# Side work admitted by an estimated clock of three engines instead of fixed allowances, in an attention and GLU block

## The chip, the cores and the metric

The kernel runs on 1 core of one Trainium2 chip. The metric is the device time of one execution in microseconds (us). A core has five engines that run side by side, each in the order in which its instructions were written: TensorE (PE in the profile; its weight loads are PEld), VectorE (DVE), ScalarE (ACT), GpSimd (POOL) and SyncE (SP, here a queue for DMAs).

## The reference, cut to what matters

```
xn = layernorm(x)                                  # x: 2048 x 576
q, k, v = heads of xn @ wqkv                       # 32 heads of 18
s = (softmax(q k^T / sqrt(18)) v) @ wo             # attention over 2048 keys
g = silu((gelu(xn @ w_gate) * (xn @ w_up)) @ w_down)   # inner width 4608
out = x + s * g
```

All inputs and outputs are float32.

## The kernel before, in words

The weight products run in float16 with each operand split into a high and a low part, and three of the four cross terms are kept. Attention runs in float16 for the scores and float32 for the exponentials times V.

**Stages.** A first stretch (to about 194 us) normalises and transposes x, projects the first heads and V and computes the first row maxima. Then comes the main loop (L1689): 16 head pairs of 64 steps, 1024 steps, each a block of TensorE work in a fixed order:

1. `qk2` (L1395): two score matmuls for the current head pair, transposed, into a PSUM tile `s`; ScalarE takes the exponential into `P` (L1405; L1407 and L1408 where the two heads have different scales).
2. `qk1` (L1342): two score matmuls for the next head pair, into another tile `s`, of which VectorE takes the row maximum into `PM` (L1350). In the loop both kinds of tile have one buffer each, so the next `qk2` waits for the exponential and the next `qk1` for the maximum.
3. Then other work, independent of these scores. It is a number of *slots* of a gate/up or q/k product (`g_run`, L1100; matmuls of L496, two at a time, 0.2158 us in the plan's prices, 27 slots a pair of products); and, in steps with `d` set, one *down stage* (`DownPair.run`, matmuls of L758, 0.735 us), half of a product with w_down. Two stages make a whole; the step with the second is called *late* in the code, since `DownPair.evac` (L769) then adds the PSUM tile `md_t` to the sum `y` on VectorE (L778). `md_t` has one buffer. A pair of products ends with a *burst* (`flush`, `burst`, L1414): the matmuls of the waiting exponentials with V, 0.86 us for a unit of four, into `md_t`, `ma_t` or `mb_t`, then added to `osb` on VectorE (L1432).

**The plan.** `make_plan` (L1610) sets, a pair of products at a time (4 to 7 steps), which steps have a down stage and how many slots each gets. Its entries are (d, slots, work in us), and 9.0 stands as the work of the last one, the burst.

**Side work.** All else is put between these steps while the program is written. `Deferred` (L38) holds functions with a due tick and a cost on the engines "A" (ScalarE), "V" (VectorE) and "G" (GpSimd); `bg` is a queue of pieces of weight preparation (`prep`, L210), with gates and rests. One call of `subtick(room, most)` (L151) is a tick: it runs what is due and fits into the room given for each engine, then up to `most` pieces from the head of `bg`, and stops at the first that doesn't fit. "T" is the step's length, by which rests and GpSimd's assumed backlog age. A piece's cost is 0.7 on VectorE or ScalarE, with few exceptions. Side work on VectorE: maxima of raw weights (L262, L267: seven for a gate/up/down chunk, five for q/k), their merge, the spread maximum (`top`, L309), and the normalisation of the attention output (L1478, L1486). On ScalarE: the copy of the up product (L672), the tanh (L690), the high part of the hidden activations (L712) and of weights (L349, L366). The copy of the gate product (L661) is written at once when a pair of products ends.

In a plain step the order is `qk2`, `qk1`, the down stage if any, the tick, in a late step then the accumulation of `y`, then the slots; so whatever VectorE work the tick of a late step admits stands ahead of `y` in VectorE's order. In a burst's step `y` comes ahead of the tick, and the burst after it.

**The allowances before.** In a plain step 0.75 on ScalarE, and on VectorE 0.75, or 0.25 where the step is late or its work is under 1.45 with fewer than 70 pieces in `bg` (L1785). In the burst's step 2.2 on ScalarE; on VectorE 0.8 if late, otherwise 2.2 in the first 256 steps and 1.5 after (L1780).

Of the kernel before, what the change touches and what calls it, by code (L numbers as in the profile page):

```python
# [23 lines left out]
NPAIR = H // 2  # L24
# [70 lines left out]
def kernel(ctx: ExitStack, tc: tile.TileContext, x, wqkv, wo, w_gate, w_up, w_down, out):  # L95
# [33 lines left out]
    defer = Deferred()  # L129
    bg = deque()  # L130
# [20 lines left out]
    def subtick(room=FREE, most=3):  # L151
        defer.advance(room)
        n = 0
        while bg and n < most:
            if isinstance(bg[0], Gate):
                if not bg[0].open():
                    return
                bg.popleft()
                continue
            if isinstance(bg[0], Rest):  # L160
                if not bg[0].over():
                    return
                bg.popleft()
                continue
            cost, fn = bg[0]
            if not defer.fits(cost):
                return
            defer.spend(cost)
            bg.popleft()
            n += 1  # L170
            if fn is None:
                return
            fn()
# [909 lines left out]
    gs = W()  # L1083
# [16 lines left out]
    def g_run(n):  # L1100


        while n > 0 and not gs.over:
            if not gs.open:
                if gs.pair is not None and blocks[0] <= gs.end:
                    return
                if gs.pair is None:
                    gs.pair = next(gstream, None)
                    if gs.pair is None:
                        gs.over = True  # L1110
                        return
                gs.pair.begin()
                gs.open = True
            n -= 1
            gs.left -= 1
            if gs.pair.slot():
                gs.open = False
                gs.end = blocks[0]
                if gs.pair.stage == 2:
                    gs.pair = None  # L1120
                    gs.closed = True
                    return
# [212 lines left out]
    def load_v(p):  # L1335
        until(lambda: vdone[0] == NT)
        v = ap.tile([P, 624], F32, tag="VT", name=f"VT{p}")
        nc.gpsimd.memset(v[:, 608:624], 0.0)
        nc.sync.dma_start(v[:, 0:608].rearrange("p (a b) -> p a b", a=NT), VS[:, :, p, :])
        VT[p] = v  # L1340
# [225 lines left out]
    pend = []  # L1566
# [4 lines left out]
    LEAD = 0  # L1571
    KEEP_HALF, KEEP_END = 2, 4
    whole = (NPAIR - 1) * 4 * NT
    dleft = [2 * NCH * NT]
    plan = deque()
    summed = False
# [68 lines left out]
    def flush(tags):  # L1645

        for tag in tags:
            if not pend:
                return
            n = next((k + 1 for k, u in enumerate(pend) if u[2] == NT - 1), len(pend))  # L1650
            burst(pend[:n], tag)
            del pend[:n]
# [36 lines left out]
    for p in range(NPAIR):  # L1689
        if p not in VT:  # L1690
            load_v(p)
        more = p + 1 < NPAIR
        for i in range(4 * NT):
            s, half = divmod(i, 2)
            qh, kt = divmod(s, NT)
            if p == NPAIR - 2:
                qh = 1 - qh
            if i == 0:
                until(lambda: mdone.get(p))
            if i == 52 and p + 2 < NPAIR:  # L1700
                load_qk(p + 2)
            kp = p + 1 if s < 30 else p + 2
            if i == 60:
                items = iter(range(64))
            pt = qk2(p, 2 * qh + half, kt, "s2" if more else ("s1", "s2")[i % 2])
            if half == 0:
                pa = pt
            else:
                pend.append((p, qh, kt, pa, pt))
            if kp < NPAIR:  # L1710
                qk1(kp, next(items))
            if i == 62 and more:
                steps[2]()
            now = 64 * p + i
            held = 2 * len(pend) + (half == 0)
            if not more and i == 32:
                tail.keep = KEEP_END
            if gs.left == 0 and gs.pair is None and not gs.closed and not plan:
                load_ohl(OUT_ORDER[0])
                u = tail.unit  # L1720
                late = False
                d = dn is not None or (
                    len(dnq) > 1 and not (more and 57 < i < 61) and held < 5 and (u is None or not u.wide)
                )
                if d:
                    if dn is None:
                        dn = DownPair()
                    late = dn.run()
                run = pend and dn is None and (held >= 6 or kt == NT - 1 and half == 1 and i < 63)
                run = run or held >= 8  # L1730
                subtick(dict(FREE, T=2.0) if not more else {"A": 0.75, "V": 0.75, "T": 2.0})
                if late:
                    dn.evac()
                    dn = None
                if run:
                    wide = u.wide if u is not None else not tail.wide
                    flush(("ma", "mb") if dn is not None or wide else ("md", "md"))
                else:
                    if gq and i % 2:
                        for fn in gq.popleft():  # L1740
                            fn()
                    if final_norm:
                        final_norm.popleft()()
                    if d or more:
                        out_run(5 if d else 10)
                    else:
                        n = 28 * max(0, len(units) - tail.keep) + (28 if tail.unit is not None else 0)
                        credit = min(credit + min(9, n / (0.75 * (32 - i % 32))), 18)
                        while credit >= 4:
                            u = tail.unit  # L1750
                            r = 14 if u is None else (u.slots - u.k) or 14
                            n = r if r <= 10 or credit >= r else (r + 1) // 2
                            n0 = tail.slots
                            out_run(n)
                            credit -= tail.slots - n0
                            if tail.unit is not None or tail.slots == n0:
                                break
            else:
                if not plan and gs.pair is None and not gs.closed:
                    plan.extend(make_plan(now, held, dn is not None, len(dnq) // 2))  # L1760
                step = plan.popleft() if plan else None
                late = False
                if step is None:
                    d = dn is not None or len(dnq) > 1 and not 58 <= i <= 60 and held < 6
                else:
                    d = step[0]
                behind = d and summed and not gs.closed
                summed = False
                if d:
                    dleft[0] -= 1  # L1770
                if d and not behind:
                    if dn is None:
                        dn = DownPair()
                    late = dn.run()
                if gs.closed:
                    gs.closed = False
                    if late:
                        dn.evac()
                        dn = None
                    subtick({"A": 2.2, "V": 0.8 if late else 2.2 if now < 256 else 1.5, "T": 0.7 + 0.86 * len(pend) + 0.73 * d}, 6)  # L1780
                    two = any(u[2] == NT - 1 for u in pend[:-1])
                    flush(("ma", "mb") if d else ("ma", "md") if two else ("md", "ma"))
                    summed = not d
                else:
                    quick = late or step is not None and step[2] < 1.45 and len(bg) < 70  # L1785
                    subtick({
                        "A": 0.75, "V": 0.25 if quick else 0.75,
                        "T": 2.0 if step is None else 0.45 + step[2],
                    })
                    if late:  # L1790
                        dn.evac()
                        dn = None
                    g_run(7 if step is None else step[1] or 0)
                    if behind:
                        dn = DownPair()
                        dn.run()
            if more and i == 60:
                steps[1]()
            if more and i == 59:
                steps = max_end(p + 1)  # L1800
                steps[0]()
# [68 lines left out]
```

## Time and profile before

| | |
|---|---|
| median of 3 runs | 2570.71 us (2570.15 to 2571.99) |
| the profiled execution, its own time | 2568.68 us |
| its span, first to last instruction | 2566.9 us |
| busy: PE, DVE, ACT, POOL | 2495.3, 1854.4, 1662.3, 1540.4 us |
| mean granted TensorE clock | 0.998 |

The page of a profile shows one execution: busy times of the engines, the chain of work that ended last, and groups of instructions by line, with the idle time of the engine just before them and what ended it. A matmul's record is longer than the distance to the next, since matmuls are pipelined: two score matmuls start together, their records last 0.38 us and the next pair starts 0.22 us later. A short stop of TensorE is therefore partly hidden by the record before it.

### The profile page before, as it was taken

How to read it: one execution, taken by the hardware profiler on the slowest of the kernel's cores; microseconds unless marked ns; L12 is line 12 of the kernel's file. 1: busy time of each engine (PE TensorE's matmuls, PEld its weight loads, DVE VectorE, ACT ScalarE, POOL GpSimd, SP SyncE). 2: the span in 40 equal slices, each digit the busy share in tenths (PEclk: the TensorE clock that was granted, in tenths of full speed). 3: DMA queues.
4: the chain of work that ended last, by engine and by line, in shares of the span. 5: the costliest groups of instructions: out<-in, count | busy, mean ns of one | idle time of the engine just before them, and what ended most of it. 6: DMA issues, size and time to landing. Idle time of an engine off the chain costs nothing.

```text
span 2566.9 us, 60550 instructions
## 1 busy us (share of the span) xinstructions
PE 2495.3 (97%) x25816; PEld 1301.0 (51%) x25816; DVE 1854.4 (72%) x2129; ACT 1662.3 (65%) x2082; POOL 1540.4 (60%) x1545
## 2 busy tenths in 40 slices
PE   7899999999999999999999999999999999999998
PEld 6554445444544454445445545454445555455555
DVE  7677768777777677777777777776777777776644
ACT  6127666766677666766666666667667666666674
POOL 4346664576357564668576675858576775767513
PEclk9999999999999999999999999999999999999999
DMA  4430111201130112111110111201111101020124
GB/s 155 133 105 11 20 54 44 75 14 32 50 88 17 22 47 60 33 39 47 20 52 15 34 38 31 55 12 36 25 38 30 38 23 44 9 51 8 41 64 139
DMA packets 134630, 118.66 MB, mean 46 GB/s; under 512 B 59690, under 2 KB 113712, under 8 KB 134361
## 3 DMA queue, kind: packets, MB, share of 16 engines
q1 hardware_dynamic: 130089, 106.39, 16.1%
q0 software_dynamic: 1568, 5.37, 0.6%
q8 instruction: 203, 3.33, 0.6%
q10 hardware_dynamic: 2704, 3.03, 0.4%
q14 instruction: 66, 0.54, 0.1%
HBM read 84.89 MB, written 29.61 MB: 45 GB/s over the span
## 4 chain that ended last, share of the span: by engine, by line
PE 84%; DVE 6%; POOL 3%; ACT 3%; DMA 2%; issue 2%; SPq 0%; ACTq 0%; POOLq 0%; DVEq 0%
PE mb_t L496 16%; PE ma_t L496 16%; PE md_t L758 15%; PE md_t L1424 10%; PE s L1399 8%; PE s L1347 8%; PE ma_t L1424 7%; DVE PM L1350 2%; ACT P L1405 1%; DMA QT<-QD 1%; DVE osb L1432 1%; POOL raw_c L356 1%; PE pv_t L515 1%; PE md_t L939 1%; PE mb_t L1424 1%
## 5 line engine op out<-in xcount | busy, mean ns | idle before, releaser
L1350 DVE TENSOR_REDUCE PM<-s 128x2 f32<-128x1024 f32 x1024 | 1251.1, 1224 | 397.2 <-PE s L1347 389.2
L1405 ACT ACTIVATE P<-s,etab 128x1024 f32<-128x1024 f32 x896 | 996.9, 1114 | 576.1 <-PE s L1399 563.2
L496 PE MATMUL ma_t<-XHT,whi_c 64*128 64x512 f16 x1440 | 541.1, 376 | 2.9 <-DVE evl L547 1.2
L496 PE MATMUL mb_t<-XHT,whi_c 64*128 64x512 f16 x1440 | 541.1, 376 | 0.5 <-DVE evl L547 0.2
L496 PE MATMUL ma_t<-XHT,wlo_c 64*128 64x512 f16 x1296 | 486.7, 376 | 0.0
L496 PE MATMUL mb_t<-XHT,wlo_c 64*128 64x512 f16 x1152 | 432.6, 375 | 0.0
L496 PE MATMUL ma_t<-XL,whi_c 64*128 64x512 f16 x1152 | 432.5, 375 | 0.0
L496 PE MATMUL mb_t<-XL,whi_c 64*128 64x512 f16 x1152 | 432.4, 375 | 0.0
L1399 PE MATMUL s<-QT,KT 56*128 56x512 f16 x2048 | 405.5, 379 | 7.5 <-ACT P L1405 3.0
L1347 PE MATMUL s<-KT,QT 54*128 54x512 f16 x2048 | 399.0, 377 | 13.0 <-DVE PM L1350 10.6
L496 PEld LDWEIGHTS <-whi_c 64*128 64x128 f16 x5184 | 273.7, 94 | 236.3 <-issue 10.9
L758 PE MATMUL md_t<-dhi_c,hhi 64*128 64x288 f16 x2304 | 343.5, 282 | 3.4 <-DVE osb L1432 1.5
L758 PE MATMUL md_t<-dhi_c,hlo 64*128 64x288 f16 x2304 | 343.1, 282 | 0.0
L758 PE MATMUL md_t<-dlo_c,hhi 64*128 64x288 f16 x2304 | 342.6, 282 | 0.0
L758 PEld LDWEIGHTS <-hhi 64*128 64x128 f16 x4608 | 245.8, 94 | 139.5 <-issue 14.5
L719 POOL TENSOR_TENSOR hlo<-gv,hhi 128x512 f16<-128x512 f32 x144 | 167.5, 1163 | 214.7 <-ACT hhi L712 210.4
L1424 PE MATMUL md_t<-P,VT 128*32 128x512 f32 x2472 | 292.1, 596 | 1.2 <-DVE ob L972 0.7
L697 POOL TENSOR_SCALAR tw<-tw 128x512 f32<-128x512 f32 x144 | 91.0, 632 | 334.2 <-ACT tw L690 333.9
L1399 PEld LDWEIGHTS <-KT 56*128 56x128 f16 x2048 | 123.9, 94 | 246.8 <-issue 157.1
L778 DVE SCALAR_TENSOR_TENSOR y<-md_t,c_c,y 128x576 f32<-128x576 f32 x272 | 219.6, 808 | 16.1 <-PE md_t L758 16.1
L684 POOL TENSOR_TENSOR tw<-gs 128x512 f32<-128x512 f32 x144 | 151.3, 1051 | 122.3 <-ACT gs L661 122.0
L496 PEld LDWEIGHTS <-wlo_c 64*128 64x128 f16 x2592 | 138.3, 94 | 120.4
(266 smaller groups left out, 3989.5 us busy)
## 6 DMA issues: line engine op xcount, KB each, us to landing
draw_c<-in_B_w_down SPq DMA_DIRECT2D x18, 576.0 KB
raw_c<-in_B_w_gate SPq DMA_DIRECT2D x18, 512.0 KB
raw_c<-in_B_w_up SPq DMA_DIRECT2D x18, 512.0 KB
obr<-rd SPq DMA_DIRECT2D x30, 256.0 KB
KT<-KD SPq DMA_DIRECT2D x32, 224.0 KB
QT<-QD SPq DMA_DIRECT2D x32, 216.0 KB
VS<-vst POOLq DMA_DIRECT2D x16, 304.0 KB, 2.7
VT<-VS SPq DMA_DIRECT2D x16, 304.0 KB
```

What stands on the lines that cost most here:

```text
L356: nc.gpsimd.tensor_scalar(raw, raw, sc, None, op0=ALU.mult)
L496: m = nc.tensor.matmul(o, lw, xx, start=self.stage == 0 and self.k == 0, stop=self.stage == 1 and self.k == self.slots - 1, skip_group_che ...
L684: gp.tensor_tensor(st["t"], st["g"], st["g"], op=ALU.mult)
L697: gp.tensor_scalar(st["t"], st["t"], 1.0, 1.0, op0=ALU.mult, op1=ALU.add)
L719: gp.tensor_tensor(hs.lo[:, ft], st["v"], hs.hi[:, ft], op=ALU.subtract)
L758: m = nc.tensor.matmul(self.t.t[:, hf, 0:288], a[r, ft, sl], b[r, ft, 288 * hf:288 * hf + 288], start=self.stage == 0 and k == 0, stop=sel ...
L778: nc.vector.scalar_tensor_tensor(yy, y, w.c, yy, op0=ALU.mult, op1=ALU.add)
L1347: nc.tensor.matmul(s1[:, h], QT[p][r, P * qt:P * qt + P], KT[p][r, 512 * kb:512 * kb + 512], start=True, stop=True)
L1350: nc.vector.tensor_reduce(PM[p][:, :, qt, kb:kb + 1], s1, op=ALU.max, axis=AX.X)
L1399: nc.tensor.matmul(s2[:, h], KT[p][r, P * kt:P * kt + P], QT[p][r, 512 * qb:512 * qb + 512], start=True, stop=True)
L1405: nc.scalar.activation(pt, s2, AF.Exp, scale=ETAB[j0])
L1424: nc.tensor.matmul(t.t[qd:qd + 32, :], VT[p][:, c0:c0 + 32], pt[:, h], start=kt == k0, stop=kt == k1, skip_group_check=True,)
```

## The change

A record `clk` holds, for the step being written, an estimate of when TensorE, VectorE and ScalarE will be done (`pe`, `dve`, `act`) and when the last row maximum and exponential end (`red`, `exp`). `clock_step` moves it over `qk2` and `qk1`. `clock_room` works out a tick's room: how long each engine may go on with side work so that the next step's exponential and row maximum still end by the time at which the step after needs their tiles, capped by `most` (1.5, in the burst's step 2.9). `clock_side` runs the tick with that room and moves the clock by what was admitted. The accumulation of `y` is charged 0.81 on VectorE, the burst's addition 0.7, the copy at a pair's end 0.69 on ScalarE. The fixed allowances, the two conditions on `now` and `len(bg)` and the `quick` rule go. The branch taken after the last gate/up pair keeps its allowances, and no matmul is added or removed.

```diff
--- before.py
+++ after.py
@@ -1571,6 +1571,34 @@
     LEAD = 0
     KEEP_HALF, KEEP_END = 2, 4
     whole = (NPAIR - 1) * 4 * NT
+    clk = W()
+    clk.pe = clk.dve = clk.act = clk.red = clk.exp = 0.0
+
+    def clock_step(exp, red):
+
+        t = max(clk.pe, clk.exp + 0.06) + 0.21
+        clk.act = clk.exp = max(clk.act, t + 0.1) + exp
+        if red:
+            t = max(t, clk.red + 0.06) + 0.22
+            clk.dve = clk.red = max(clk.dve, t + 0.15) + 1.23
+        clk.pe = t
+
+    def clock_room(work, after, dve, act, most):
+
+        end = clk.pe + work + 0.43 + after
+        return {
+            "A": min(most, end - 1.18 - max(clk.act, clk.pe - 0.3) - act),
+            "V": min(most, end + 0.21 - 1.29 - max(clk.dve, clk.pe - 0.3) - dve),
+            "T": 0.43 + work,
+        }
+
+    def clock_side(room, most):
+
+        a, v = room["A"], room["V"]
+        subtick(room, most)
+        clk.act = max(clk.act, clk.pe - 0.3) + a - defer.room["A"]
+        clk.dve = max(clk.dve, clk.pe - 0.3) + v - defer.room["V"]
+
     dleft = [2 * NCH * NT]
     plan = deque()
     summed = False
@@ -1712,6 +1740,7 @@
             if i == 62 and more:
                 steps[2]()
             now = 64 * p + i
+            clock_step(1.12 if 2 * p // 7 == (2 * p + 1) // 7 else 1.38, kp < NPAIR)
             held = 2 * len(pend) + (half == 0)
             if not more and i == 32:
                 tail.keep = KEEP_END
@@ -1777,23 +1806,30 @@
                     if late:
                         dn.evac()
                         dn = None
-                    subtick({"A": 2.2, "V": 0.8 if late else 2.2 if now < 256 else 1.5, "T": 0.7 + 0.86 * len(pend) + 0.73 * d}, 6)
+                    work = 0.3 + 0.86 * len(pend) + 0.73 * d
+                    clock_side(clock_room(work, 1.5, 0.81 * late + 0.7, 0.0, 2.9), 6)
                     two = any(u[2] == NT - 1 for u in pend[:-1])
                     flush(("ma", "mb") if d else ("ma", "md") if two else ("md", "ma"))
+                    clk.pe += work
+                    clk.dve = max(clk.dve + 0.81 * late, clk.pe) + 0.7
                     summed = not d
                 else:
-                    quick = late or step is not None and step[2] < 1.45 and len(bg) < 70
-                    subtick({
-                        "A": 0.75, "V": 0.25 if quick else 0.75,
-                        "T": 2.0 if step is None else 0.45 + step[2],
-                    })
+                    work = 1.5 if step is None else step[2]
+                    nxt = plan[0][2] if plan else 1.5
+                    if nxt == 9.0:
+                        nxt = 2.9
+                    clock_side(clock_room(work, nxt, 0.81 * late, 0.0, 1.5), 3)
                     if late:
                         dn.evac()
                         dn = None
+                        clk.dve = max(clk.dve, clk.pe + 0.73) + 0.81
                     g_run(7 if step is None else step[1] or 0)
                     if behind:
                         dn = DownPair()
                         dn.run()
+                    clk.pe += work
+                    if gs.closed:
+                        clk.act = max(clk.act, clk.pe) + 0.69
             if more and i == 60:
                 steps[1]()
             if more and i == 59:
```

## The prediction

> **What bounds the kernel now.** I read the page first: the busy times, then the chain that ended last.
>
> ```profile
> span 2566.9 us, 60550 instructions
> PE 2495.3 (97%) x25816; PEld 1301.0 (51%) x25816; DVE 1854.4 (72%) x2129; ACT 1662.3 (65%) x2082; POOL 1540.4 (60%) x1545
> PE 84%; DVE 6%; POOL 3%; ACT 3%; DMA 2%; issue 2%; SPq 0%; ACTq 0%; POOLq 0%; DVEq 0%
> ```
>
> TensorE bounds it: 97% busy and 84% of the chain. The change touches no matmul and only reorders what VectorE and ScalarE do beside them, so all it can win or lose is idle time of TensorE. The view by windows gives that for the stretch in which the change acts, from the first main-loop step (about 194 us) to the end of the gate/up pairs (about 2400 us); columns are the stretch, its length, and busy time with counts of PE, PEld, DVE, ACT and POOL.
>
> ```profile
> 194.00:2400.00 2206.00, 2178.17 (x22424) 1096.27 (x22425) 1637.49 (x1793) 1495.86 (x1845) 1410.28 (x1400) 1.00 0.14 35
> ```
>
> TensorE idles 2206.00 - 2178.17 = 27.8 us there, at granted clock 1.00. The view of waits, for the same stretch, names whom TensorE waited for.
>
> ```profile
> PE s L1347 <- DVE PM L1350: 9.1, 15, 1.8
> PE ma_t L1424 <- ACT gs L661: 3.2, 8, 0.4
> PE s L1399 <- ACT P L1405: 2.5, 6, 0.6
> PE s L1399 <- ACT P L1408: 2.4, 3, 1.2
> PE s L1399 <- DVE PM L1350: 1.3, 1, 1.3
> PE md_t L758 <- DVE y L778: 1.1, 3, 0.4
> ```
>
> A late row maximum (PM) costs 9.1 + 1.3 us, a late exponential (P) 2.5 + 2.4 us: 15.3 us together. These are the waits that better admission could remove; it is the bound of the gain on view. The wait for y, which matters below, is small now: 1.1 us in three places. No row names a weight piece (L349, L357), so having the weights ready sooner wins nothing by itself.
>
> **What the new rule admits.** The durations of what shares the two engines, from the groups by line of the stretch (VectorE) and of the whole run (ScalarE):
>
> ```profile
> L1350 DVE TENSOR_REDUCE PM<-s 128x2 f32<-128x1024 f32 x947 | 1159.4, 1224 | 370.6 <-PE s L1347 363.3
> L778 DVE SCALAR_TENSOR_TENSOR y<-md_t,c_c,y 128x576 f32<-128x576 f32 x260 | 209.9, 807 | 0.0
> L262 DVE TENSOR_REDUCE m_c<-raw_c 128x1 f32<-128x512 f32 x85 | 55.2, 673 | 0.0
> L267 DVE TENSOR_REDUCE m_c<-draw_c 128x1 f32<-128x576 f32 x34 | 24.7, 744 | 0.0
> L1478 DVE TENSOR_TENSOR osb<-osb,obr 128x512 f32<-128x512 f32 x29 | 26.5, 913 | 0.0
> L1486 DVE TENSOR_TENSOR onl<-osb,onh 128x512 f16<-128x512 f32 x29 | 24.3, 839 | 0.0
> L1405 ACT ACTIVATE P<-s,etab 128x1024 f32<-128x1024 f32 x896 | 996.9, 1114 | 576.1 <-PE s L1399 563.2 <-PE s L1347 7.2 <-PE md_t L939 0.7
> L690 ACT ACTIVATE tw<-tw 128x512 f32<-128x512 f32 x144 | 89.7, 623 | 6.5 <-POOL tw L686 6.5
> ```
>
> The clock's prices (1.23 for a reduction, 0.81 for y, 1.12 for an exponential) agree with these rows. With all engines on time the clock has the reduction end 1.38 us after the row-max matmuls, so the room on VectorE is work + next + 0.43 + 0.21 - 1.29 - 1.38 = work + next - 2.03, less 0.81 in a "late" step, one that ends with a y accumulation; the cap is 1.5. On ScalarE it is work + next - 1.75. A side operation is charged 0.7. So:
> - Plain step of 7 slots (1.51) before another: V 0.99, one operation; old V 0.75, one. Equal.
> - Short steps (1.08, 1.08): V 0.13, A 0.41: none; the old rule let one ScalarE operation through.
> - First half of a down pair (1.60) before its second (2.03): V 1.5, two; old 0.75, one.
> - Late step of 2.03 before 1.60: V 0.79, one; old 0.25, none.
> - Late step of 1.81 just before a burst: the burst counts as 2.9, V = 1.81 + 2.9 - 2.84 = 1.87, capped to 1.5: two; old 0.25, none.
> - Burst with three units (2.88): V 1.65, two; old 2.2 (three) in the first 256 steps and 1.5 (two) after.
>
> **What it saves.** First the early bursts. VectorE, then TensorE, around 751 us:
>
> ```profile
> 748.09 1.86 DVE L262 TENSOR_REDUCE m_c<-raw_c 128x1 f32<-128x512 f32 x3
> 749.86 0.68 DVE L1432 TENSOR_TENSOR osb<-md_t,osb 128x512 f32<-128x512 f32 x1
> 750.46 1.22 DVE L1350 TENSOR_REDUCE PM<-s 128x2 f32<-128x1024 f32 x1
> ```
> ```profile
> 750.01 0.38 PE L496 MATMUL mb_t<-XL,whi_c 64*128 64x512 f16 x1
> 750.50 0.39 PE L1399 MATMUL s<-QT,KT 56*128 56x512 f16 x2
> 751.73 0.39 PE L1347 MATMUL s<-KT,QT 54*128 54x512 f16 x2 [0.83 <-DVE PM L1350]
> ```
>
> Three maxima in one burst push the burst's sum (osb) and the reduction back, and the next row-max matmuls wait 0.83 us. With two, 1.86 / 3 = 0.62 us of it goes. I find five such places before step 256 and take 3 us for them. Second, ScalarE operations in short steps:
>
> ```profile
> 1656.69 1.27 POOL L686 TENSOR_TENSOR tw<-tw,gs 128x512 f32<-128x512 f32 x1
> ```
> ```profile
> 1657.99 0.63 ACT L690 ACTIVATE tw<-tw 128x512 f32<-128x512 f32 x1 [1.01 <-POOL tw L686]
> 1658.53 1.10 ACT L1405 ACTIVATE P<-s,etab 128x1024 f32<-128x1024 f32 x1
> ```
> ```profile
> 1659.67 0.39 PE L1399 MATMUL s<-QT,KT 56*128 56x512 f16 x2 [0.44 <-ACT P L1405]
> ```
>
> The tanh stands in ScalarE's queue until GpSimd has its input, the exponential queues behind it, TensorE idles 0.44 us. Where a short step now denies it, it comes a step later and waits for less. Three such places and some with gs and gv: 3 us. One more for small operations of the weight preparation: **7 us saved** in all; bounds 0 and the 15.3 us above. Those that stay are plan, DMA and row-max ends, which the clock doesn't price.
>
> **What it costs.** The late steps. VectorE, then TensorE, in a pair whose last step is late (its plan price 1.81) before a burst that opens with a down stage:
>
> ```profile
> 1320.97 1.23 DVE L1350 TENSOR_REDUCE PM<-s 128x2 f32<-128x1024 f32 x1 [0.59 <-PE s L1347]
> 1322.11 0.81 DVE L778 SCALAR_TENSOR_TENSOR y<-md_t,c_c,y 128x576 f32<-128x576 f32 x1
> 1323.22 1.23 DVE L1350 TENSOR_REDUCE PM<-s 128x2 f32<-128x1024 f32 x1 [0.30 <-PE s L1347]
> 1324.36 0.24 DVE L1467 RECIPROCAL oc<-oc 128x16 f32<-128x16 f32 x1
> 1324.52 1.22 DVE L262 TENSOR_REDUCE m_c<-raw_c 128x1 f32<-128x512 f32 x2
> ```
> ```profile
> 1322.58 0.38 PE L1399 MATMUL s<-QT,KT 56*128 56x512 f16 x2
> 1322.80 0.38 PE L1347 MATMUL s<-KT,QT 54*128 54x512 f16 x2
> 1323.02 0.28 PE L758 MATMUL md_t<-dhi_c,hhi 64*128 64x288 f16 x2
> ```
>
> y directly follows the reduction and ends at 1322.92; the next down stage, which writes the one buffer (md_t) that y reads, starts at 1323.02. The slack is 0.10 us. Side work is emitted ahead of y in VectorE's queue. Two maxima there take 1.22 us (row at 1324.52), y ends that much later, and the in-order TensorE stands for about 1.22 - 0.10 = 1.1 us at the stage, with every score matmul behind it. The clock holds room only for the reduction, never for md_t; the old 0.25 kept these steps clear. Over the run 232 of the y are followed by a down stage (the timeline, y by y), 173 of them with under 0.6 us between, and the commonest value is this 0.1.
>
> How often? The plans that the program writes before have 154 pairs; 63 end in a late step with md_t needed next and room for two (41%). There are 21 weight preparations with some eight VectorE operations each, spread by the new rooms over about seven steps, so each meets about one such step: 21 x 0.41 = 8.6; I take 8 x 1.1 = 9 us. The 58 normalisation operations (29 + 29 by their rows) and 21 "top" reductions come singly; 117 of 960 steps are late, tight and with room: 79 x 0.12 = 9.6, at about 0.4 us each (0.61 less 0.31 of slack in a 2.03 step, more for an L1478) 4 us. **Cost 13 us**; bounds: 0, if the work finds room before those steps, and 25 us, if all 63 + 54 places (54: the 2.03 steps) cost a fifth of a microsecond on average.
>
> The rest costs nothing: "T" differs by 0.02 to 0.07 us a step, and it only ages rests and GpSimd's assumed backlog; neither DMA issues nor queues are moved but by a step or two. Without that cover it is one DMA wait of some 2 us, either way.
>
> **Sum.** 13 - 7 = +6 us on the profiled execution's 2568.68 us, whose span is 2566.9 (1.8 lie around it): 2574.7. That execution is 2.0 under the median of the runs, 2570.71; on the median's scale it is **2577 us**.
>
> **The rivals.** A measurement of this kernel can tell about 0.2%, 5.1 us, from no change.
>
> (a) Slower, as above: 2577, up to 2590 with more collisions. For it: the 0.10 us slack and a price that the clock leaves out. Against: a first-half step just before takes two operations, and its lag then closes the late step.
>
> (b) Faster: the side work nearly always finds the roomier first-half steps and bursts, y stays clear, and 7 to 10 us of the 15.3 remain won: 2562, at the bound 2555. It decides from under 2 us of new waits for y.
>
> (c) No change: the two terms meet, or the clock, which is fed by nothing that happens on the chip and leaves out the row-max ends and the q/k evacuations, decides much as the constants did: 2571.
>
> (d) Slower by fixed prices. The normalisation's operations are charged 0.7 us, but the view of one line shows them (ns, least/median/most) far above at times; so is a small one of the row-max end:
>
> ```profile
> L1478 DVE TENSOR_TENSOR osb<-osb,obr x30: 679/835/1644, 307.3 to 2454.4; 128x512 f32<-128x512 f32 x30
> L1363 DVE SCALAR_TENSOR_TENSOR rmc<-rmx,rmc x16: 191/193/1117, 181.1 to 2422.5; 128x32 f16<-128x32 f32 x16
> ```
>
> By means the excess is 29 x (0.913 - 0.7) + 29 x (0.839 - 0.7) = 10 us of VectorE. Half of it exposed, because the clock fills the steps to their edge, with the savings kept small at 2 us and y's term at 3, gives 2571 + 5 - 2 + 3 = 2577. [...]
>
> **How the numbers follow.** (a) 0.38, (d) 0.10, (c) 0.27, (b) 0.25: slower 0.48, same 0.27, faster 0.25. The range runs from the middle of the faster case, 2561, to 2590, the sum with y's term at its bound (+25 - 7 = +18, rounded up).
>
> **What would show it.** Right: TensorE's and its weight loads' waits for y (L758, L1424) grow to some 8 us or more, with maxima directly ahead of y in VectorE's order, the waits for PM fall to 5 or 6 us, and the tanh waits less. Wrong: y's wait stays near 1 us and idle time falls under 22 us: then (b). If all waits stay within 3 us of these rows, (c). If the two-input operations stand ahead of late reductions, (d).

## The result, and the profile after

The changed kernel is slower by 2.9%: a median of 2646.27 us (2644.19 to 2648.35, 4 runs) against 2570.89 us (2570.15 to 2571.99, 4 runs), ratio 1.0294 with a 95% interval of 1.0282 to 1.0305. The forecast was 2577 us with a range that ended at 2590. The side was right and the size was not: 75 us came where 6 were worked out. The profiled execution of after took 2644.19 us.

First the page of after: span, busy times, the shares of the chain, and the costliest wait of GpSimd.

```profile
span 2642.4 us, 60547 instructions
PE 2515.4 (95%) x25816; PEld 1339.5 (51%) x25816; DVE 1845.0 (70%) x2129; ACT 1658.7 (63%) x2082; POOL 1534.6 (58%) x1545
PE 82%; DVE 7%; ACT 6%; DMA 2%; issue 2%; POOL 1%; ACTq 0%; POOLq 0%; SPq 0%; DVEq 0%
L697 POOL TENSOR_SCALAR tw<-tw 128x512 f32<-128x512 f32 x144 | 91.3, 634 | 455.8 <-ACT tw L690 455.6
```

The work is the same to within three instructions, and no engine's busy time moved by more than 3%. In the chain ScalarE's share doubled, from 3% to 6%. GpSimd waits 455.6 us for the tanh (L690); in the page of before the same row has

```profile
L697 POOL TENSOR_SCALAR tw<-tw 128x512 f32<-128x512 f32 x144 | 91.0, 632 | 334.2 <-ACT tw L690 333.9
```

So ScalarE's side work comes later than it did; in the kernel with gv free, below, the same wait is 375.2 us, so most of the rise goes with the late copies. In the view by windows, the main stretch of after (columns as in the prediction) idles 2206.00 - 2129.09 = 76.9 us of TensorE instead of 27.8, and gets 21754 matmuls done in it instead of 22424.

```profile
194.00:2400.00 2206.00, 2129.09 (x21754) 1097.92 (x21755) 1581.42 (x1746) 1448.54 (x1795) 1362.31 (x1361) 1.00 0.14 35
```

TensorE's waits over the whole run of after say for whom (us in total, times, longest):

```profile
PE mb_t L496 <- ACT gv L672: 41.7, 29, 2.0
...
PE md_t L758 <- DVE y L778: 5.7, 10, 1.2
PE s L1347 <- DVE PM L1350: 5.3, 11, 0.7
PE ma_t L1424 <- ACT gs L661: 5.0, 8, 1.9
PE s L1399 <- ACT P L1405: 3.2, 9, 0.9
...
PE md_t L1424 <- DVE y L778: 2.7, 2, 1.5
```

The first row is a new wait; among those who waited for L672 in before, the view of that line has

```profile
  PE mb_t L496: 0.2, 1
```

Now the first matmul of a gate/up pair into mb_t stands until ScalarE has copied the pair before out of that buffer (gv, L672). Twenty-nine such stops, 41.7 us, are more than half of the 75 us lost. The wait for y grew as predicted, from 1.1 to 5.7 + 2.7 us, and the wait for PM fell as predicted, from 10.6 to 5.3 us (whole run).

One of the 29 in the order of time, ScalarE and then TensorE of after:

```profile
332.71 0.69 ACT L661 ACTIVATE gs<-ma_t,uE_c 128x512 f32<-128x512 f32 x1 [0.61 <-PE ma_t L496]
333.30 1.11 ACT L1405 ACTIVATE P<-s,etab 128x1024 f32<-128x1024 f32 x1
334.30 0.63 ACT L712 ACTIVATE hhi<-gv 128x512 f16<-128x512 f32 x1
335.97 0.27 ACT L1371 ACTIVATE rms<-md_t 64x128 f16<-64x128 f16 x1 [1.04 <-PE md_t L1369]
...
336.78 1.11 ACT L1405 ACTIVATE P<-s,etab 128x1024 f32<-128x1024 f32 x1 [0.55 <-PE s L1347]
337.79 0.68 ACT L672 ACTIVATE gv<-mb_t,uE_c 128x512 f32<-128x512 f32 x1
```
```profile
336.31 0.38 PE L496 MATMUL ma_t<-XHT,whi_c 64*128 64x512 f16 x1
338.52 0.37 PE L496 MATMUL mb_t<-XHT,whi_c 64*128 64x512 f16 x1 [1.84 <-ACT gv L672]
```

The same pair in before, ScalarE:

```profile
334.39 1.11 ACT L1405 ACTIVATE P<-s,etab 128x1024 f32<-128x1024 f32 x1
335.39 0.63 ACT L712 ACTIVATE hhi<-gv 128x512 f16<-128x512 f32 x1
335.91 0.68 ACT L672 ACTIVATE gv<-mb_t,uE_c 128x512 f32<-128x512 f32 x1
```

In before, hhi (L712) and gv are both written in the burst's tick. In after the tick holds hhi only; ScalarE then stands idle for 1.04 us, and gv is written a tick later, behind the next exponential. TensorE stops 1.84 us for it. The chip had the room; the clock's number for it was too small by 0.01 us. In a burst of two units the work is 0.3 + 2 x 0.86 = 2.02, its end lies 2.02 + 0.43 + 1.5 = 3.95 after the matmuls, ScalarE is 1.38 ahead by the clock (gs with 0.69 and an exponential with 1.12, less the 0.43 that TensorE itself moves on), so the room is 3.95 - 1.18 - 1.38 = 1.39. Two operations are charged 1.40.

The program's own order of writing says how often: in 29 pairs of after gv comes one tick late (25) or two (4), in none of before. The rooms of those ticks are 1.39 in 16 cases and 0.41 to 1.36 in the others. In 25 of the 29 hhi is in the tick ahead of gv. That is hardly new: hhi shares the first tick of gv in 31 of the 144 pairs of before and in 36 of after. New is the room: before, the burst's constant 2.2 held three operations.

### The profile page after: what moved, and what is told of

It is laid out like the page before. It is cut to its first block, busy times and chain, and to the rows that moved or that the text cites. A ratio compares the mean times of both kernels' runs of the same rounds, so it can differ in the third digit from the quotient of the medians.

```text
span 2642.4 us, 60547 instructions
## 1 busy us (share of the span) xinstructions
PE 2515.4 (95%) x25816; PEld 1339.5 (51%) x25816; DVE 1845.0 (70%) x2129; ACT 1658.7 (63%) x2082; POOL 1534.6 (58%) x1545
## 4 chain that ended last, share of the span: by engine, by line
PE 82%; DVE 7%; ACT 6%; DMA 2%; issue 2%; POOL 1%; ACTq 0%; POOLq 0%; SPq 0%; DVEq 0%
PE mb_t L496 16%; PE ma_t L496 15%; PE md_t L758 15%; PE md_t L1424 9%; PE s L1399 8%; PE ma_t L1424 8%; PE s L1347 7%; DVE PM L1350 2%; ACT P L1405 2%; ACT gv L672 1%; PE mb_t L939 1%; DMA mxd_j<-mx_j 1%; DMA md<-rms 1%; PE mc_t L515 1%; PE pv_t L515 1%
## 5 line engine op out<-in xcount | busy, mean ns | idle before, releaser
L496 PEld LDWEIGHTS <-whi_c 64*128 64x128 f16 x5184 | 289.9, 94 | 273.4 <-issue 58.2
L1399 PE MATMUL s<-QT,KT 56*128 56x512 f16 x2048 | 419.9, 380 | 7.1 <-ACT P L1405 3.2
L1347 PE MATMUL s<-KT,QT 54*128 54x512 f16 x2048 | 412.6, 378 | 8.0 <-DVE PM L1350 5.3
L758 PE MATMUL md_t<-dhi_c,hhi 64*128 64x288 f16 x2304 | 364.9, 284 | 8.9 <-DVE y L778 5.7
L758 PE MATMUL md_t<-dhi_c,hlo 64*128 64x288 f16 x2304 | 364.6, 283 | 0.0
L758 PE MATMUL md_t<-dlo_c,hhi 64*128 64x288 f16 x2304 | 364.2, 283 | 0.0
L697 POOL TENSOR_SCALAR tw<-tw 128x512 f32<-128x512 f32 x144 | 91.3, 634 | 455.8 <-ACT tw L690 455.6
L758 PEld LDWEIGHTS <-hhi 64*128 64x128 f16 x4608 | 264.1, 94 | 137.9 <-issue 27.1
L1424 PE MATMUL md_t<-P,VT 128*32 128x512 f32 x2160 | 256.7, 597 | 5.7 <-DVE y L778 2.7
L1399 PEld LDWEIGHTS <-KT 56*128 56x128 f16 x2048 | 131.6, 94 | 247.7 <-issue 164.5
L1424 PE MATMUL ma_t<-P,VT 128*32 128x512 f32 x1816 | 210.7, 596 | 7.9 <-ACT gs L661 5.0
```

The costliest lines, as they stand in the source:

```text
L496: m = nc.tensor.matmul(o, lw, xx, start=self.stage == 0 and self.k == 0, stop=self.stage == 1 and self.k == self.slots - 1, skip_group_che ...
L697: gp.tensor_scalar(st["t"], st["t"], 1.0, 1.0, op0=ALU.mult, op1=ALU.add)
L758: m = nc.tensor.matmul(self.t.t[:, hf, 0:288], a[r, ft, sl], b[r, ft, 288 * hf:288 * hf + 288], start=self.stage == 0 and k == 0, stop=sel ...
L1347: nc.tensor.matmul(s1[:, h], QT[p][r, P * qt:P * qt + P], KT[p][r, 512 * kb:512 * kb + 512], start=True, stop=True)
L1399: nc.tensor.matmul(s2[:, h], KT[p][r, P * kt:P * kt + P], QT[p][r, 512 * qb:512 * qb + 512], start=True, stop=True)
L1424: nc.tensor.matmul(t.t[qd:qd + 32, :], VT[p][:, c0:c0 + 32], pt[:, h], start=kt == k0, stop=kt == k1, skip_group_check=True,)
```

## The experiments

The theory, G: late copies of gv cost about 64 of the 75 us; the prediction's y costs the rest. The rivals: that the loss is the late y alone, as predicted, and bigger; that it is the fixed prices of side work, rival (d) of the prediction; that it is the clock on one of the two engines as such; and, called P in the expectations, that the later tanh makes worse plans. Each ratio is to the kernel before on the same chip, with its 95% interval. Medians of before there were 2567.31 us (first four kernels), 2569.10 (next four) and 2568.39 (last four). Where gv is written freely the line numbers behind L663 are greater by 4.

**gv at its tick, whatever the room** (after; the price is still charged):

```diff
-            defer.at(defer.now + 1, lambda: up(u), on_act())
+            def gv():
+                defer.spend(on_act())
+                up(u)
+
+            defer.at(defer.now + 1, gv)
```

> The changed kernel, with the copy of the up product (gv, L672) written at its tick whatever ScalarE's room is; its 0.7 is still charged. Theory G: the loss is mostly this copy, which the clock puts off in 29 pairs, so that the next pair's first matmul into mb_t waits (41.7 us idle, and about 0.16 us more hidden in each by the record before it: 46 us). It gives 2646 - 46 = 2600 us, and the wait of TensorE for gv gone. Theory Y (the recorded prediction: side work ahead of y in late steps, 13 us) gives 2646 or a little less. Theory P (the lag of the tanh changes the plans, and the plans are worse) gives 2646, since the tanh still lags.

Measured 2578.52 us, 1.0043 (1.0028 to 1.0058): 2.51% of 2569, 64.5 us, came back with this one edit, more than the 46 us expected. The row for mb_t is gone; what leads in the main loop now is y:

```profile
PE md_t L1428 <- DVE y L782: 6.8, 8, 1.7
PE md_t L762 <- DVE y L782: 6.1, 11, 1.1
...
PE s L1351 <- DVE PM L1354: 4.8, 12, 0.7
```

**A burst's ScalarE room greater by 0.06** (after):

```diff
-                    clock_side(clock_room(work, 1.5, 0.81 * late + 0.7, 0.0, 2.9), 6)
+                    room = clock_room(work, 1.5, 0.81 * late + 0.7, 0.0, 2.9)
+                    room["A"] += 0.06
+                    clock_side(room, 6)
```

> The changed kernel, with 0.06 us more room on ScalarE in the burst's tick and nothing else. A burst of two units has 1.39 us of room by the clock, two operations cost 1.40, and where the high part of the hidden activations (0.7) is due in the same tick the copy gv is put off. Theory G: 23 of the 29 late copies go, 23/29 x 46 = 36 us: 2610 us, and TensorE's wait for gv falls to 6 places and some 9 us. Theory Y: 2646. Theory P: 2646.

Measured 2601.31 us, 1.0130 (1.0115 to 1.0146). Six hundredths of a microsecond in a number of the planner gave back 1.64%, 42 us, where 36 were expected. Six late copies are left, those whose room was lower still. The kernel with gv free is another 0.87% (22 us) faster; the gaps between TensorE's blocks, as in the table further down, put 10.8 us of it on mb_t and 5 us on the out-projection:

```profile
PE mb_t L496 <- ACT gv L672: 7.6, 6, 1.9
```

**No maxima ahead of y** (after):

```diff
-                    clock_side(clock_room(work, nxt, 0.81 * late, 0.0, 1.5), 3)
+                    room = clock_room(work, nxt, 0.81 * late, 0.0, 1.5)
+                    if late:
+                        room["V"] = min(room["V"], 0.25)
+                    clock_side(room, 3)
```

> The changed kernel, with VectorE's room in late plain steps capped at the old 0.25, so that y is not queued behind side work. Theory Y: 13 us less, 2633 us, and the waits for y (5.7 and 2.7 us in the page's view) back to about 1. Theory G: 8 us less at most, 2638 to 2646, since the late copies stay (42 us of waits). Theory P: 2646.

Measured 2636.31 us, 1.0267 (1.0250 to 1.0284). The wait for y falls from 5.7 to 0.8 us, the 41.7 us for gv stay to the digit:

```profile
PE mb_t L496 <- ACT gv L672: 41.7, 29, 2.0
...
PE md_t L758 <- DVE y L778: 0.8, 3, 0.3
```

So y is 0.27 of the 2.94 percentage points, some 7 us, as theory G allowed, and not the size of the loss.

**Both edits**, gv free and y clear:

> Both edits together. If G and Y are the whole and add: 2646 - 46 - 10 = 2590 us. If the plans are worse (P), a rest of 15 us or more over the kernel before stays though neither wait is left: 2586 or above. If there is nothing else: 2571 to 2580.

Measured 2571.68 us, 1.0015 (1.0006 to 1.0025). From the kernel with gv free alone that is 0.28%, again 7 us for y. The two edits add, hardly anything of the change's loss is left, and theory P falls. TensorE's idle time in the main stretch is 2206.00 - 2177.51 = 28.5 us, against 36.2 with gv free alone (second view):

```profile
194.00:2400.00 2206.00, 2177.51 (x22408) 1103.09 (x22408) 1627.96 (x1792) 1490.49 (x1844) 1406.24 (x1398) 1.00 0.14 36
```
```profile
194.00:2400.00 2206.00, 2169.78 (x22327) 1099.79 (x22327) 1620.53 (x1786) 1484.72 (x1837) 1400.95 (x1395) 1.00 0.14 35
```

**ScalarE by the clock, VectorE by the old constants** (after; of the edit, here and in the next, only the lines that set the room):

```diff
+                    room["V"] = 0.8 if late else 2.2 if now < 256 else 1.5     # burst
+                    quick = late or step is not None and step[2] < 1.45 and len(bg) < 70
+                    room["V"] = 0.25 if quick else 0.75                        # plain step
```

> The changed kernel with VectorE's rooms put back to the old constants; ScalarE's rooms by the clock. The order that it writes has 18 late copies gv (29 in the changed kernel). Theory G, at the 64/29 = 2.2 us that a late copy cost in the pair of the changed kernel and e1: 40 us over the kernel before, ratio 1.015; at the 1.6 us of the wait alone 29 us, 1.011. Theory Y (VectorE is what matters beyond that): the waits for y at the level of before. Rival: the loss needs both rooms together, ratio under 1.005.

Measured 2617.63 us, 1.0184 (1.0169 to 1.0200), with 18 late copies. That is 48.5 us, above the 40 us of theory G; the rival falls. What the other 8 us are is open; the wait for PM, with one stop of 3.6 us, is 1.2 us above that of before:

```profile
PE mb_t L496 <- ACT gv L672: 25.8, 18, 2.4
PE s L1347 <- DVE PM L1350: 11.8, 17, 3.6
```

**VectorE by the clock, ScalarE by the old constants** (after):

```diff
+                    room["A"] = 2.2      # burst
+                    room["A"] = 0.75     # plain step
```

> The changed kernel with ScalarE's rooms put back to the old 2.2 and 0.75; VectorE's by the clock. No copy is late in the order that it writes. Theory G: the big loss is gone; what stays is Y, 7 us by the pair e1 and e4: 1.003. [...]

Measured 2586.55 us, 1.0065 (1.0050 to 1.0080), with no late copy: above the 1.003 of theory G. Late reductions, the sign of rival (d), are missing: the wait for PM is 6.1 us, under the 10.6 of before. y leads the waits of the main loop:

```profile
PE md_t L1424 <- DVE y L778: 7.8, 9, 1.6
...
PE md_t L758 <- DVE y L778: 4.2, 10, 1.0
```

The two halves sum to 2.49%, the whole is 2.94%: with both rooms by the clock the program writes another order, and 29 copies are late instead of 18.

**The late copy put into the kernel before:**

```diff
-subtick({"A": 2.2, ...
+subtick({"A": 1.39 if len(pend) == 2 and not d else 2.2, ...
```

> The kernel before with one constant changed: ScalarE's room is 1.39 instead of 2.2 in the tick of a burst of two units without a down stage, which is what the clock gives there. The order that it writes has 19 late copies, no clock, no other edit. Theory G: 19 x 1.6 = 30 us to 19 x 2.2 = 42 us: ratio 1.012 to 1.016, with waits of some 27 us for gv. If the late copy is only a mark of something else that the clock does: 1.000 to 1.003.

Measured 2609.52 us, 1.0152 (1.0137 to 1.0167). There is no clock in this kernel, only the number 1.39 in one kind of tick. It makes 19 late copies, all in ticks with hhi ahead of gv, and costs 2609.52 - 2569.10 = 40.4 us, 2.1 us each, as theory G has it. No short step refuses anything here that it took before. After has 64.5 us on 29, 2.2 us each.

```profile
PE mb_t L496 <- ACT gv L672: 25.3, 19, 1.8
```

**VectorE by the clock, y clear** (VectorE's clock alone, as above, with the edit for y):

> As e6, with late plain steps capped at 0.25 on VectorE: the clock decides only VectorE's other steps. If the tanh that the clock puts off is what is left in e4 (1.0015), this is 1.000 or below; the early bursts' saving, 3 us by the prediction, would give 0.999. If VectorE's fuller steps cost by themselves: 1.002 or above.

Measured 2572.33 us, 1.0013 (1.0003 to 1.0022). Against 1.0065 that is 0.52%, 13.4 us for y where no copy is late, with an interval of some 5 us either way. It lies between the two cases that were expected, 1.000 and 1.002, and decides for neither.

```profile
PE s L1347 <- DVE PM L1350: 7.2, 13, 1.1
```

**Before, with its early bursts at 1.5 as the later ones** (`2.2 if now < 256 else 1.5` becomes `1.5`):

> The kernel before with VectorE's allowance in the first 256 steps' bursts at 1.5, as it is later, instead of 2.2: the prediction's first saving alone, 3 us, ratio 0.999, with the wait of 0.83 us at 751 us of the profile before gone. Rival: the maxima move to other steps and cost the same there, 1.000.

Measured 2567.65 us, 1.0000 (0.9991 to 1.0009). The wait for PM falls from 10.6 to 8.5 us, and the time does not move, as the rival has it. Up to 800 us the five waits of L1347 for PM, 3.3 us, are gone, that at 751 us among them, but the waits for osb (L1369) grow from 1.6 to 3.1 us there.

```profile
PE s L1347 <- DVE PM L1350: 8.5, 13, 1.5
```

**After, gv free, and y written ahead of the side work of a late step** (the edit of gv is the first above; this is the other):

```diff
-                    clock_side(clock_room(work, nxt, 0.81 * late, 0.0, 1.5), 3)
+                    room = clock_room(work, nxt, 0.81 * late, 0.0, 1.5)
                     if late:
                         dn.evac()
                         dn = None
                         clk.dve = max(clk.dve, clk.pe + 0.73) + 0.81
+                    clock_side(room, 3)
```

> The changed kernel with the copy gv as in e1, and in late plain steps y written ahead of the tick, so that the side work that the clock admits stands behind y. Theory: what the clock lacked is the two deadlines, those of mb_t and md_t; with both kept by order instead of by a cap, this is at or below e4 (1.0015), 0.999 to 1.0015. Rival: side work behind y makes the next reduction late instead, waits for PM over 7 us, 1.003 or more.

Measured 2566.66 us, 0.9994 (0.9985 to 1.0003): the best of all kernels tried, and not to be told from before. It admits by the clock with all its prices and the side work of late steps, and none of the loss is left.

```profile
194.00:2400.00 2206.00, 2179.80 (x22462) 1097.57 (x22460) 1631.18 (x1794) 1494.63 (x1848) 1408.98 (x1402) 1.00 0.14 36
```

TensorE idles 26.2 us in the main stretch, 1.6 less than in before. That is all that the clock wins on view, and it does not show in the time.

**Before, y first,** so that late steps may take side work by the old constants (0.75, or 0.25 in short steps):

> The kernel before with y ahead of the tick in late plain steps, and these steps with 0.75 on VectorE where they had 0.25 for being late. If the room of late steps is worth having once y is safe, 0.998 to 1.000; if the next reduction comes late instead, 1.001 to 1.003. There was no need for room in the profile before (no weight piece was waited for), so 1.000 is the likeliest.

Measured 2576.67 us, 1.0032 (1.0019 to 1.0044). No change had been called the likeliest; it is the case of late reductions. Side work behind y delays the next reduction, and this constant does not see it. The wait for PM grows from 10.6 to 14.0 us; the rest of the 8 us this row does not show:

```profile
PE s L1347 <- DVE PM L1350: 14.0, 24, 1.5
```

**VectorE by the clock, y first:**

> As e6 (VectorE by the clock, ScalarE by the old constants), with y ahead of the tick in late plain steps. Beside e6 (1.0065) and e8 (1.0013): order instead of a cap gives 0.999 to 1.0015 if the wait for y was all of e6's loss; 1.004 or more if the work ahead of y was not what cost.

Measured 2570.14 us, 1.0008 (0.9999 to 1.0017), with the wait for PM at 7.9 us in 16 places. Between this kernel and the one above only VectorE's rooms differ ("T" aside): the clock's rooms put side work into late steps without the late reductions of the constants. For VectorE's reductions the clock does here what it was written for.

## Why the prediction failed in size

Start-to-start gaps of TensorE's blocks, over the duration that each kind of block takes undisturbed, place the time. They are worked out from the starts in the timeline (us, number of late places in brackets; a name pair is the block before and the block after the gap):

```
gap                                  before  after       gv free  y clear  both
gate/up slots to slots (mb_t)           0.9  46.4 (30)       1.3     48.2   1.5
scores to down stage (y)                4.4  12.0           12.4      5.0   4.6
scores to burst                        15.1  17.3           22.8     14.9  16.2
second scores to first (PM)            17.8  13.2           10.8     13.3  13.0
down stage to burst, and in the burst  11.8  18.2           12.0     18.3  12.1
slots to second scores                 10.4  12.3           10.1     12.0  12.9
out-projection at the end               0.6   6.3            0.6      6.1   0.6
all gaps                               96.4 164.5          105.3    157.2  96.1
```

**The step that failed** is the sentence "The rest costs nothing", and ahead of it the list of rooms, which has the burst on VectorE alone. ScalarE's room in a burst of two units fell from 2.2 to 1.39 us, by the formulas of the diff, so that two operations no longer fit; the prediction gave this no term. What falls out of the tick is gv, whose lateness stops TensorE. The kernel before with the one number 1.39 shows that this is enough: 19 late copies and 40.4 us with the old allowances everywhere else. The sentence "Where a short step now denies it, it comes a step later and waits for less" is true as far as it goes: ScalarE's idle time for GpSimd's input of the tanh fell from 6.5 us in 12 places to 1.6 us in 3. But it asks what the denied operation waits for, and not what then waits for it. How many of the 29 late copies come from such denials is not shown; hhi stands in gv's tick little more often than before (36 pairs against 31).

The row that could have warned was in the trace of before: mb_t is a single buffer that gv has to free before the next pair, with 0.2 us of wait in one place. The gaps above put 45 us on it (46.4 - 1.3), 5.7 us on the out-projection (late only in kernels whose last pair's copy is late), 6 us ahead of and in bursts and 2 to 3 us each on the two kinds of scores; at the way from scores to burst the kernel with gv free is 5.5 us worse. The sums differ by 59.2 of the 64.7 us between the two spans (2642.4 and 2577.7); 5.5 us these gaps do not place. What ties the whole to the late copies is the edit of gv and its counterpart in the kernel before, 64.5 us on 29 copies and 40.4 us on 19.

**The cost of y** was right in mechanism. Its size, 13 us, was measured as 13.4 us with VectorE's clock alone, as 7 us within the whole change and again as 7 us without the late copies. Each of these differences has an interval of some 5 us either way, so it is not shown that they differ, and the close hit is in part luck. The rows show such a place, VectorE and TensorE of after:

```profile
1267.77 1.23 DVE L1350 TENSOR_REDUCE PM<-s 128x2 f32<-128x1024 f32 x1
1268.92 1.40 DVE L267 TENSOR_REDUCE m_c<-draw_c 128x1 f32<-128x576 f32 x2
1270.23 0.81 DVE L778 SCALAR_TENSOR_TENSOR y<-md_t,c_c,y 128x576 f32<-128x576 f32 x1
```
```profile
1269.56 0.43 PE L1347 MATMUL s<-KT,QT 54*128 54x512 f16 x2
1271.10 0.30 PE L758 MATMUL md_t<-dhi_c,hhi 64*128 64x288 f16 x2 [1.11 <-DVE y L778]
```

Two maxima directly ahead of y, and the down stage stands 1.11 us; the prediction said about 1.1. The places are only in part those of the sum, which had most of the cost at the down stage: with VectorE's clock alone 4.2 us of the waits for y stand there and 7.8 us at the burst's matmuls into md_t (L1424). In the trace of before a down stage is the next to write md_t behind 216 of the y, not 232; the 173 with under 0.6 us between are there.

**The savings** were read from the right rows and do not show in the time. The wait for PM did fall to the 5 to 6 us foretold, but the two kernels that bring it down without a loss elsewhere gain 0.0% (early bursts, interval 0.09% either way, 2.3 us) and 0.06% (gv free and y first, interval from -0.15% to +0.03%). Of the 7 us at most 4 can be there net of what else these kernels change; the sign stays open. The 1.0043 that is left without the late copies is 7 us of y and 4 us that stay with y kept clear (1.0015); they are gone when y is written first (0.9994), and by what is not settled.

**The rivals.** Rival (a) named the right side by the smaller of two mechanisms. Without the late copies the side would have come out as forecast too (1.0043), largely by y; that +11 us stand there beside the forecast +6 is partly luck, since the 7 us of savings in that sum are not seen. The other 64.5 of the 75 us come from a term that the prediction had at nothing. Rival (d), fixed prices, is not supported: the best kernel charges the same 0.7 for every operation and stands at 0.9994. Its largest row is uneven in after too (L1478 from 676 to 1445 ns; 679 to 1644 in before); no run isolates it or shows what makes it so. Rivals (b) and (c) fell with the late copies; with gv free and y kept clear or first the outcome is that of (c), 1.0015 and 0.9994. The range took its upper end from y's bound (117 places at a fifth of a microsecond are 23 us, not 25, which changes little); a bound for deferred ScalarE work was missing, and each copy that TensorE waits for costs some 2 us.

## What to carry to other kernels

A rule that admits side work by the room to the engines' next deadlines treats all side work as equal; an operation that frees a single buffer has a deadline of its own, so write it whatever the room, or ahead of the rest, and let the others wait. When constants become formulas, work out the room of each kind of step on each engine and hold it against sums of the prices (1.39 against 1.40), since a hundredth of a microsecond on paper decided some 2 us on the chip, 16 times. And judge a deferral by what waits for the deferred work, not by its own slack.

## What the runs showed of the hardware

In after, a stop of TensorE of 2.02 us, up to 695.07 us, was followed by half clock. The view by windows up to shortly behind the stop's end, behind that, and behind that again (the third number from the end is the granted clock):

```profile
692.40:695.60 3.20, 1.18 (x11) 0.57 (x9) 1.91 (x3) 2.94 (x6) 1.07 (x1) 1.00 0.18 40
695.60:699.20 3.60, 3.60 (x32) 2.97 (x29) 0.98 (x1) 2.05 (x5) 3.46 (x4) 0.53 0.06 16
699.20:702.00 2.80, 2.80 (x35) 2.26 (x32) 2.27 (x3) 1.73 (x3) 2.63 (x4) 1.00 0.00 0
...
2317.00:2320.60 3.60, 3.60 (x31) 3.16 (x29) 0.82 (x1) 1.11 (x1) 3.51 (x4) 0.53 0.78 200
...
2514.60:2518.20 3.60, 3.60 (x36) 2.67 (x32) 0.23 (x1) 2.50 (x3) 0.67 (x1) 0.56 0.02 5
```
```profile
695.07 0.37 PE L496 MATMUL mb_t<-XHT,whi_j 64*126 64x512 f16 x1 [2.02 <-ACT gv L672]
```

Over the 3.6 us from 695.60 the mean of the granted clock was 0.53, and over the 3.4 us from 695.65 to 699.05 us 0.51. The last two rows are the other such stretches in the loop and the end of after, behind a stop of 1.88 us for gv and one of 1.83 us in the out-projection. The three cost at most 3.6 x (0.47 + 0.47 + 0.44) = 5.0 us, part of which lies in the gaps above. In before the clock stood at 1.00 from 194 to 2560 us. Of the four runs of the kernel before with late copies, two had a mean granted clock of 0.996 (2610.62 and 2611.09 us), one of 0.997 (2608.43) and one of 0.998 (2606.63); so a small part of what the late copies cost, by these runs at most some 5 of 40.4 us, may be this.

It does not follow from the stop alone: in after another stop of 2.02 us for gv, up to 1771.77 us, was followed by a clock of 1.00; and the stop of 1.84 us at 338.5 us was followed by full clock in after, and a stop of the same 1.84 us at the same place of the kernel with y clear by half clock. The three in this order:

```profile
1771.60:1775.20 3.60, 3.43 (x43) 2.63 (x44) 1.20 (x2) 1.54 (x4) 3.43 (x4) 1.00 0.06 14
```
```profile
338.50:342.00 3.50, 3.48 (x44) 2.70 (x45) 1.46 (x2) 1.51 (x2) 3.42 (x5) 1.00 0.02 5
```
```profile
339.90:343.40 3.50, 3.50 (x29) 2.95 (x25) 1.23 (x1) 1.51 (x2) 2.60 (x4) 0.52 0.01 5
```

Nor do TensorE's busy times up to the ends of the two stops of 2.02 us tell them apart: 1.18 us of 3.2 in both (691.87 to 695.07 us and 1768.57 to 1771.77 us). What decides is not shown.
